# Key-value sums with the features stationary in four column groups, and small matmuls in groups of 32 tokens

## The chip, the core and the metric

The kernel runs on one core of one Trainium2 chip. The metric is the device time of one execution in microseconds; the figure for the kernel before is the median of three runs. A core has TensorE (PE, with its weight loads shown apart as PEld), VectorE (DVE), ScalarE (ACT), GpSimd (POOL) and SyncE (SP, which issues the transfers here). They run at the same time and wait for one another by semaphores.

## The reference

Two stages. The first is a linear attention over 4 batches, 4 heads, 1088 tokens and 32 dimensions. Each key and query is projected twice to 8 numbers, and the outer product of the two gives 64 features per head. The second is a gated feed-forward layer over all 4352 tokens, 128 wide, 2048 hidden.

```
phi(x)[i*8+j] = (S1 x)[i] * (S2 x)[j]          # 64 features per head
kv  = sum over tokens of phi(k) v^T            # 64 x 32 per batch and head
z   = sum over tokens of phi(k)                # 64 per batch and head
x   = (phi(q) kv) / (phi(q) z + 1e-6)
h   = x @ w_in ;  g = h * clip(h + 3, 0, 6) / 6 ;  out = g @ w_out
```

## The kernel before

**The feed-forward layer** takes most of the time. Tokens come in chunks of 512 (`CHUNKS`, eight of them and a last of 256), hidden features in pairs of 128-wide tiles. A step (`step`) multiplies a chunk by one pair of tiles of `w_in`. Both operands are split into a high and a low part, and three products are added: `L810` high by high, `L811` and `L816` the two cross terms. ACT adds 3 and clips below (`L823`), DVE clips above and multiplies (`L826`), ACT rounds to the high part (`L830`), and POOL or DVE subtracts to get the low part (`L834`). Three more products (`L855`, `L856`, `L858`) add the step to the output chunk. These six matmuls, 128 by 128 by 512, are called main matmuls below.

**The attention** feeds it. Per batch, the keys come in two groups of four and five tiles of 128 tokens (`KGROUPS`). `features` projects them: `L462` takes 64 tokens at a time as the stationary operand, two column groups of TensorE's array per tile, with the 64 projection columns moving. ACT copies the result (`L471`), DVE or POOL forms the outer products (`L490`).

Then the sums over the tokens (`keys`). Batch 0 (`b < DIRECT`) uses `kv_direct`, `L546`: a head's 64 features are stationary, in two column groups of 64, and 33 columns of v move, 32 of them the values and the last a column of ones, so that the 33rd result is z. Batches 1 to 3 use `kv`, `L561`: 32 columns of v are stationary, one column group of 32 per head, and the head's 64 features move, which gives kv turned on its side. For these batches z comes another way. `zz` (`L575`) sums the outer product of the two projections over all pairs of heads, `twice` copies kv and this product to SBUF on ACT (`L579`, `L581`), `turn` transposes kv (`L585`) and spreads the product to 128 partitions (`L588`, two matmuls with `spread` stationary), and `z` on DVE multiplies by a 0/1 matrix `pickT` and adds along the row (`L593`, `L596`). `spread` and `pickT` are made once near the start by `picks`, `turn_picks` and `copy_picks` (`L514`, `L516`, `L521`, `L524`). `halves` copies the result into `kvb[b]` on ACT (`L620`).

**The queries.** The first two chunks (`c < NEAR`) are transposed on TensorE (`L716`, copied at `L722`), the later ones (`far_queries`) by DVE and two transfers through DRAM; their projection is `L467`. The quotient is `nd` in `divided` (`L644`): 64 tokens at a time stationary, in two column groups, against `kvb`; DVE divides (`L651`, `L653`, `L655`). Then x is turned (`L672` or `L776`), and split (`L685`, `L689`).

**The order.** All of this is laid down as operations with an estimated cost per engine, a due time and the buffers they hold. `Plan.order` walks through modelled time and puts on each engine, whenever it is free, the ready operation with the earliest due time; the order that comes out is emitted as each engine's fixed queue. The due times are `when` and `xneed` minus the numbers in `LEADS`, `DUES`, `LOAD_DUE` and so on. Until `FILL_UNTIL` the plan puts filler matmuls (`L337`) where TensorE would be idle. An operation that may run on POOL or DVE is placed by `choose`, with `HOLD`, `SOON` and `PATIENCE`.

An fp32 matmul shows in the trace as two weight loads and two matmuls, so 144 rows of `L462` keys are 72 calls.

Of the kernel before, what the change touches and what calls it, by code (L numbers as in the profile page):

```python
# [15 lines left out]
F32 = mybir.dt.float32  # L16
# [3 lines left out]
ALU = mybir.AluOpType  # L20
# [56 lines left out]
BUFS = dict(h=2, o=2, a=2, raw=4, kT=3, v=3, qT=3, ab=3, kph=2, qph=2, phT=2, x=2, xh=5, g=5, gh=4, gl=4, os=2, part=4, cv=2, den=2, rden=2, xturn=1, xT=2, own=1, z=1, kvT=1)  # L77
ANY = ("a", "h", "o")

DIRECT = 1  # L80
# [7 lines left out]
DUES = (103.17, -33.21, 264.39, 135.8)  # L90
LAG = 103.99
W_DUE = (-192.19, 97.55, -48.18, 47.22, 162.42, -80.89, -2.9, 95.45)
CONV_LEAD = (-95.46, -154.15, 221.22, 172.43, 163.86, -1.9, 118.07, 58.88, -1.91)
LOAD_DUE = {'kT_0': -98.0, 'wiraw0': -99.0, 'kT_1': -96.0, 'kT_3': -92.0, 'qT_1': -95.0, 'v_3': -89.0, 'v_0': -93.0, 'qT_0': -97.0, 'v_1': -94.0, 'woraw0': -91.0, 'v_2': -88.0, 'kT_2': -87.0, 'wiraw1': -90.0}
LEADS = ({'ab': 12.96, 'cp': -82.47, 'ph': 183.6, 'kv': 105.14, 'kvb': 263.66, 'tr': 8.1, 'trcp': -338.67, 'nd': -150.04, 'norm': -67.61, 'xt': 144.32, 'xh': -299.21, 'xl': 20.48, 'k0': -50.53, 'kld': 93.74, 'vld': -73.42, 'qld': -227.7, 'rd': 94.61, 'xw': 73.75, 'xr': 86.41, 'sum': 208.48}, {'ab': 78.08, 'cp': 355.85, 'ph': -42.74, 'kv': 21.15, 'kvb': -73.24, 'tr': -268.31, 'trcp': -123.46, 'nd': -4.6, 'norm': 104.98, 'xt': 7.02, 'xh': -59.73, 'xl': 215.84, 'k0': 17.93, 'kld': -11.45, 'vld': 94.8, 'qld': 37.13, 'rd': 150.19, 'xw': 265.05, 'xr': -157.89, 'sum': -169.58}, {'ab': -313.33, 'cp': -208.9, 'ph': 497.08, 'kv': -430.54, 'kvb': 92.37, 'tr': 61.5, 'trcp': 1.64, 'nd': 28.0, 'norm': 109.69, 'xt': 35.9, 'xh': -102.84, 'xl': -39.8, 'k0': 445.75, 'kld': 300.46, 'vld': -93.89, 'qld': -26.76, 'rd': 164.41, 'xw': -289.67, 'xr': -28.97, 'sum': 42.05})


PICKS = 12.0


HOLD = 2.46
HOLD_DUE = -94.44
# [203 lines left out]
def fused_kernel(ctx: ExitStack, tc: tile.TileContext, qT, kT, v1, sb, w_in, w_out, outT):  # L306
# [18 lines left out]

    spread = const.tile([P, H, R, R], F32, name="spread")
    pickT = const.tile([P, 2, Q], F32, name="pickT")
# [122 lines left out]
    def features(src, n, name, tag, due, ld, srcb, psb, eng_cost, LEAD, far=False):  # L450


        T = {}
        pb, abb, phb = Buf(psb), Buf(("ab",)), Buf((tag,))
        T["abb"], T["n"] = abb, n

        def mm(_):
            T["ps"] = bank(pb.tag, f"abps_{name}")
            for t in range(n):
                out = T["ps"][:, : n * AB].rearrange("p (s x) -> p s x", s=2)[:, :, t * Q : (t + 1) * Q]  # L460
                for e in (0, HP):
                    nc.tensor.matmul(out[e : e + HP], src[0][:, t * P + e : t * P + e + HP], s_ab.rearrange("p s h r -> p s (h r)"), start=True, stop=True)  # L462
# [29 lines left out]
        if far:  # L492
            o1 = plan.add({PE: 0.1 + 0.121 * n}, due - LEAD["ab"], [ld], mm_far, [srcb, pb, abb], 256 * n, S_READY)
            o2 = plan.add({DVE: 0.12 + 0.067 * n}, due - LEAD["cp"], [o1], cp_far, [pb, abb])
        else:
            o1 = plan.add({PE: 0.11 + 0.115 * n}, due - LEAD["ab"], [ld], mm, [srcb, pb, abb], 256 * n, S_READY)
            o2 = plan.add({ACT: 0.06 + 0.0535 * n}, due - LEAD["cp"], [o1], cp, [pb, abb])
# [11 lines left out]
    turned = {}  # L509

    def picks(_):
        eye = ident[:Q, :Q].rearrange("k (h r) -> k h r", r=R)
        for e in range(0, P, Q):
            nc.scalar.copy(spread[e : e + Q], ident[e : e + Q, e : e + Q].rearrange("k (h r) -> k h r", r=R).unsqueeze(3).broadcast_to([Q, H, R, R]))  # L514
        turned["pick"] = buf("x", [P, 4, DM], "pick")[:Q, :2, :].rearrange("k t (h r s) -> k (t h) r s", r=R, s=R)
        nc.scalar.copy(turned["pick"], eye.unsqueeze(2).broadcast_to([Q, H, R, R]))  # L516

    def turn_picks(_):
        turned["ps"] = bank(pickb.tag, "pick_ps")
        for p in range(2):  # L520
            nc.tensor.transpose(turned["ps"][:, p * Q : (p + 1) * Q], turned["pick"][:, 2 * p : 2 * p + 2].rearrange("k h i j -> k (h i j)"), ident[:Q, :Q])  # L521

    def copy_picks(_):
        nc.scalar.copy(pickT, turned["ps"][:, : 2 * Q].rearrange("p (a x) -> p a x", a=2))  # L524

    pickb, turnedb = Buf(ANY), Buf(("x",))
    a = plan.add({ACT: 0.66}, PICKS, [], picks, [turnedb])
    a = plan.add({PE: 0.2}, PICKS, [a], turn_picks, [pickb, turnedb], 64)
    pick_op = plan.add({ACT: 0.16}, PICKS, [a], copy_picks, [pickb])

    def keys(b, due, psbs, ph_eng):
# [6 lines left out]
        def kv_direct(_, t, i, T, vbox):  # L538
# [4 lines left out]
            for h in range(H):  # L543
                w = slice(h * DV, (h + 1) * DV)
                e = F * (h % 2)
                nc.tensor.matmul(  # L546
                    K["ps"][e : e + F, w],
                    T["ph"][:rows, t, h * F : (h + 1) * F],
# [7 lines left out]
        def kv(_, t, i, T, vbox):  # L556

            if i == 0:
                K["ps"] = bank(kvbuf.tag, f"kvps_{b}")
            for h in range(H):  # L560
                nc.tensor.matmul(  # L561
                    K["ps"][h * D : (h + 1) * D, :F],
                    vbox[0][:, t, h * DV : h * DV + D],
                    T["ph"][:, t, h * F : (h + 1) * F],
                    start=i == 0,
                    stop=i == KT - 1,
                    tile_position=(0, h * D),
                )

        def zz(_, n, i0, T):  # L570

            for t in range(n):
                a, b_ = (T["ab"][:, x + t * Q : x + (t + 1) * Q] for x in (0, n * Q))
                e, i = t % 4 * Q, i0 + t
                nc.tensor.matmul(K["ps"][e : e + Q, Z0 : Z0 + Q], a, b_, start=False, stop=i >= KT - 4, skip_group_check=True, tile_position=(0, e))  # L575

        def twice(_):
            K["kvT"] = buf("kvT", [P, 2, F], f"kvT_{b}")
            nc.scalar.copy(K["kvT"], K["ps"][:, :F].unsqueeze(1).broadcast_to([P, 2, F]))  # L579
            K["z"] = buf("z", [P, Q], f"z_{b}")  # L580
            nc.scalar.copy(K["z"], K["ps"][:, Z0 : Z0 + Q])  # L581

        def turn(_):

            nc.tensor.transpose(K["ps"][:, P : 2 * P], K["kvT"].rearrange("p a f -> p (a f)"), ident)  # L585
            for p in range(2):
                at = Z0 + Q + p * Q
                nc.tensor.matmul(K["ps"][:, at : at + Q], spread[:, 2 * p : 2 * p + 2].rearrange("k h i j -> k (h i j)"), K["z"], start=True, stop=True)  # L588

        def z(_):  # L590

            own = buf("own", [P, 2, Q], f"own_{b}")
            nc.vector.tensor_tensor(own, K["ps"][:, Z0 + Q : Z0 + 3 * Q].rearrange("p (a x) -> p a x", a=2), pickT, op=ALU.mult)  # L593
            for u in range(2):
                at = u * DV + D
                nc.vector.tensor_reduce(kvb[b][u * F : (u + 1) * F, :, at : at + 1], own[u * F : (u + 1) * F], axis=mybir.AxisListType.X, op=ALU.add)  # L596

        for half in range(2):
# [5 lines left out]
            T, o3, phb = features(kbox, n, f"k{g}", "kph", d, lk, kb, psbs[half], ph_eng[half], LEAD)  # L604
            for t in range(n):
                i = t0 + t - b * KT
                mm = kv_direct if b < DIRECT else kv
                prev = plan.add({PE: 0.25 if b < DIRECT else 0.135}, d - LEAD["kv"] + 0.3 * t, [o3[t], lv, prev], partial(mm, t=t, i=i, T=T, vbox=vbox), [phb, vb, kvbuf], 528)
            if b >= DIRECT:
                prev = plan.add({PE: 0.1 + 0.04 * n}, d - LEAD["kv"] + 0.3 * n, [prev], partial(zz, n=n, i0=t0 - b * KT, T=T), [T["abb"], kvbuf], 32 * n)  # L610

        def halves(_):
            for e in (0, F):
                if b >= DIRECT:
                    at = P + e // F * D
# [328 lines left out]
```

## Time and profile before

| | us |
|---|---|
| median of three runs | 243.69 (243.48 to 243.83) |
| profiled execution | 244.41 |
| its span on the core | 242.3 |
| PE busy | 235.5 |
| DVE busy | 189.2 |
| ACT busy | 166.1 |
| POOL busy | 138.1 |

The span is the time from the first to the last instruction that the profiler saw; the profiled execution's own time holds 2.1 us more around it. Busy time is the time in which at least one instruction of the engine was running. A matmul's end is modelled, so the distance between the starts of two matmuls says more than their durations. The chain of waits follows the work that ended last back from the end: to what released an instruction, or to the instruction before it on its engine.

### The profile page before, as it was taken

What the parts mean: (1) busy time and instruction counts of PE and PEld (TensorE: products, weight loads), DVE (VectorE), ACT (ScalarE), POOL (GpSimd) and SP (SyncE); (2) the same over time, 40 slices, a digit from 0 to 9 for tenths busy, and PEclk for the clock granted to TensorE, in tenths of its full rate; (3) what the DMA queues carried; (4) which work ended last, traced back from release to release, by engine and by line L of the source; (5) the groups of instructions that cost most, each with busy time, mean ns of one, the idle gap of its engine ahead of it and who ended that gap; (6) DMA issues with size and microseconds to landing.
All of it is one profiled execution on the core that took longest, in us unless ns stands there. A gap on an engine that the chain in (4) does not pass through costs nothing.

```text
span 242.3 us, 4487 instructions
## 1 busy us (share of the span) xinstructions
PE 235.5 (97%) x1742; PEld 182.7 (75%) x1744; DVE 189.2 (78%) x261; ACT 166.1 (69%) x216; POOL 138.1 (57%) x86
## 2 busy tenths in 40 slices
PE   8998999999999989999999999999999999999994
PEld 3786767867767767787777777888788878888894
DVE  3899999999999999885664968766846495768771
ACT  6664798748756265689875865685678577768671
POOL 2734999966999936029976431254359704425400
PEclk9999999999999999999999999999999999999999
DMA  6998922014249965640000111410130010001010
GB/s 200 387 391 287 351 92 91 0 16 157 80 121 261 282 167 175 161 144 0 3 0 0 43 43 47 91 39 3 43 87 0 3 43 0 0 3 43 0 43 23
DMA packets 18004, 23.75 MB, mean 98 GB/s; under 512 B 1728, under 2 KB 11072, under 8 KB 17984
## 3 DMA queue, kind: packets, MB, share of 16 engines
q1 hardware_dynamic: 17984, 23.48, 30.7%
q8 instruction: 13, 0.21, 0.3%
q14 instruction: 7, 0.06, 0.1%
HBM read 16.26 MB, written 7.21 MB: 97 GB/s over the span
## 4 chain that ended last, share of the span: by engine, by line
PE 89%; DVE 8%; ACT 1%; issue 1%; DVEq 0%
PE o L855 13%; PE h L810 13%; PE o L856 13%; PE o L858 12%; PE h L816 12%; PE h L811 12%; PE nd L644 3%; PE warm L337 3%; DVE g L826 2%; PE abps_k L462 2%; PE kvps L561 2%; DVE gl L834 1%; PE abps_q L467 1%; PE kvps L546 1%; PE phps L716 1%
## 5 line engine op out<-in xcount | busy, mean ns | idle before, releaser
L834 POOL TENSOR_TENSOR gl<-g,gh 128x1024 fp32r<-128x1024 f32 (+1 forms) x42 | 100.2, 2399 | 73.4 <-ACT gh L830 28.5
L826 DVE SCALAR_TENSOR_TENSOR g<-g,h 128x1024 f32<-128x1024 f32 (+1 forms) x72 | 82.4, 1155 | 33.0 <-ACT g L823 31.7
L823 ACT ACTIVATE g<-h 128x1024 f32<-128x1024 f32 (+1 forms) x72 | 70.0, 978 | 32.2 <-PE h L816 21.2
L830 ACT CAST gh<-g 128x1024 fp32r<-128x1024 f32 (+1 forms) x72 | 72.0, 1001 | 24.6 <-PE o L856 18.3
L810 PE MATMUL h<-xh,wi_hi 128*128 128x512 f32 (+1 forms) x144 | 56.5, 393 | 1.9 <-DVE g L826 1.6
L855 PE MATMUL o<-gh,wo_hi 128*128 128x512 f32 (+1 forms) x144 | 55.6, 388 | 0.0
L811 PE MATMUL h<-xh,wi_lo 128*128 128x512 f32 (+1 forms) x144 | 55.0, 382 | 0.0
L816 PE MATMUL h<-xl,wi_hi 128*128 128x512 f32 (+1 forms) x144 | 55.0, 384 | 0.0
L856 PE MATMUL o<-gh,wo_lo 128*128 128x512 f32 (+1 forms) x144 | 54.6, 382 | 0.0
L858 PE MATMUL o<-gl,wo_hi 128*128 128x512 f32 (+1 forms) x144 | 43.7, 385 | 0.0
L834 DVE TENSOR_TENSOR gl<-g,gh 128x1024 fp32r<-128x1024 f32 (+1 forms) x30 | 36.2, 1214 | 5.6 <-ACT gh L830 5.3
L810 PEld LDWEIGHTS h<-xh,wi_hi 128*128 128x128 f32 x144 | 27.0, 187 | 10.0 <-DVE g L826 2.0
L855 PEld LDWEIGHTS o<-gh,wo_hi 128*128 128x128 f32 x144 | 27.0, 188 | 6.6 <-ACT gh L830 0.5
L816 PEld LDWEIGHTS h<-xl,wi_hi 128*128 128x128 f32 x144 | 27.0, 188 | 5.8
L856 PEld LDWEIGHTS o<-gh,wo_lo 128*128 128x128 f32 x144 | 27.0, 188 | 5.3
L811 PEld LDWEIGHTS h<-xh,wi_lo 128*128 128x128 f32 x144 | 27.0, 188 | 5.0
L858 PEld LDWEIGHTS o<-gl,wo_hi 128*128 128x128 f32 x144 | 26.0, 188 | 5.6
L490 POOL TENSOR_TENSOR ph_k<-ab_k 128x512 f32<-128x512 f32 (+1 forms) x15 | 14.6, 988 | 11.0 <-ACT ab_k L471 11.0
L490 POOL TENSOR_TENSOR ph_q<-ab_q 128x512 f32<-128x512 f32 x14 | 16.8, 1218 | 4.1 <-DVE ab_q L475 2.0
L644 PEld LDWEIGHTS nd<-kvb,phT 128*64 128x64 f32 x272 | 9.2, 137 | 4.0 <-issue 2.7
L644 PE MATMUL nd<-kvb,phT 128*64 128x66 f32 x272 | 11.0, 226 | 0.0
L748 DVE STREAM_TRANSPOSE pht<-ph_q 128x1024 f32<-128x1024 f32 (+1 forms) x7 | 8.1, 1158 | 0.1
(87 smaller groups left out, 171.5 us busy)
## 6 DMA issues: line engine op xcount, KB each, us to landing
phd<-pht SPq DMA_DIRECT2D x24, 128.0 KB, 3.5
phT<-phd SPq DMA_DIRECT2D x6, 512.0 KB, 4.4
wiraw<-w_in_dram SPq DMA_DIRECT2D x4, 512.0 KB, 6.9
qT<-qT_dram SPq DMA_DIRECT2D x8, 256.0 KB, 5.8
woraw<-w_out_dram SPq DMA_DIRECT2D x4, 512.0 KB, 5.4
outT_dram<-os SPq DMA_DIRECT2D x8, 256.0 KB, 2.0
xd<-xt SPq DMA_DIRECT2D x24, 64.0 KB, 1.9
xT<-xd SPq DMA_DIRECT2D x6, 256.0 KB, 2.8
```

What stands on the lines that cost most here:

```text
L490: engines[e].tensor_tensor(out, a_, b_, op=ALU.mult)
L644: nc.tensor.matmul(W["nd"][e : e + HP, o : o + 2 * DV], T["phT"][:, p, i : i + HP], kvb[batch_of(c0 + i)][:, p, :], start=True, stop=True)
L810: nc.tensor.matmul(T["h"][:, u, :n], wi_hi[:, f], x, start=True, stop=False)
L811: nc.tensor.matmul(T["h"][:, u, :n], wi_lo[:, f], x, start=False, stop=False)
L816: nc.tensor.matmul(T["h"][:, u, :n], wi_hi[:, f], x, start=False, stop=True)
L823: nc.scalar.activation(T["g"][:, :, :n], T["h"][:, :, :n], AF.Relu, bias=3.0, scale=1.0)
L826: nc.vector.scalar_tensor_tensor(T["g"][:, :, :n], T["g"][:, :, :n], 6.0, T["h"][:, :, :n], op0=ALU.min, op1=ALU.mult)
L830: nc.scalar.copy(T["gh"][:, :, :n], T["g"][:, :, :n])
L834: engines[e].tensor_tensor(T["gl"][:, :, :n], T["g"][:, :, :n], T["gh"][:, :, :n].bitcast(F32), op=ALU.subtract)
L855: nc.tensor.matmul(o, wo_hi[:, f], T["gh"][:, u, :n], start=first and u == 0, stop=False)
L856: nc.tensor.matmul(o, wo_lo[:, f], T["gh"][:, u, :n], start=False, stop=False)
L858: nc.tensor.matmul(o, wo_hi[:, f], T["gl"][:, u, :n], start=False, stop=last and u == 1)
```

## The change

All batches now use one form of the sums over the tokens. A head's 64 features are stationary in two halves of 32, so that four column groups of 32 are used, and the 33 columns of v with the ones move. One token tile takes eight calls in place of four. `DIRECT`, `kv_direct`, `zz`, `twice`, `turn`, `z`, the pick matrices and their buffers (`own`, `z`, `kvT`) are gone, and `halves` is the same for all batches.

The keys of batches 1 to 3 and the quotients of chunks 2 to 8 take 32 tokens at a time in four column groups, where they took 64 in two; batch 0's keys, all of `L462`'s queries and the first two chunks' quotients stay as they are. The planner's costs of these operations are changed, and all of its due times, leads and holds; among the loads, qT_0 goes from third to tenth place and woraw0 from ninth to last of the thirteen named ones. The copies of the projections and the outer products of the features are not changed.

```diff
-STEP = 6.61
-DUES = (103.17, -33.21, 264.39, 135.8)
-LAG = 103.99
+STEP = 4.6
+DUES = (154.74, -15.16, 342.66, 122.47)
+LAG = 20.51
...
-LOAD_DUE = {'kT_0': -98.0, 'wiraw0': -99.0, 'kT_1': -96.0, 'kT_3': -92.0, 'qT_1': -95.0, 'v_3': -89.0, 'v_0': -93.0, 'qT_0': -97.0, 'v_1': -94.0, 'woraw0': -91.0, 'v_2': -88.0, 'kT_2': -87.0, 'wiraw1': -90.0}
+LOAD_DUE = {'kT_0': -98.0, 'wiraw0': -99.0, 'kT_1': -97.0, 'kT_3': -89.0, 'qT_1': -96.0, 'v_3': -95.0, 'v_0': -94.0, 'qT_0': -90.0, 'v_1': -93.0, 'woraw0': -87.0, 'v_2': -88.0, 'kT_2': -92.0, 'wiraw1': -91.0}
...
-HOLD = 2.46
+HOLD = 21.82
...
-    def features(src, n, name, tag, due, ld, srcb, psb, eng_cost, LEAD, far=False):
+    def features(src, n, name, tag, due, ld, srcb, psb, eng_cost, LEAD, far=False, w=HP):
...
-                for e in (0, HP):
-                    nc.tensor.matmul(out[e : e + HP], src[0][:, t * P + e : t * P + e + HP], s_ab.rearrange("p s h r -> p s (h r)"), start=True, stop=True)
+                for e in range(0, P, w):
+                    nc.tensor.matmul(out[e : e + w], src[0][:, t * P + e : t * P + e + w], s_ab.rearrange("p s h r -> p s (h r)"), start=True, stop=True)
...
-        def kv_direct(_, t, i, T, vbox):
+        def kv(_, t, i, T, vbox):
...
-            for h in range(H):
+            for h, f in product(range(H), range(0, F, Q)):
                 w = slice(h * DV, (h + 1) * DV)
-                e = F * (h % 2)
+                e = F * (h % 2) + f
                 nc.tensor.matmul(
-                    K["ps"][e : e + F, w],
-                    T["ph"][:rows, t, h * F : (h + 1) * F],
+                    K["ps"][e : e + Q, w],
+                    T["ph"][:rows, t, h * F + f : h * F + f + Q],
                     vbox[0][:rows, t, w],
...
-            T, o3, phb = features(kbox, n, f"k{g}", "kph", d, lk, kb, psbs[half], ph_eng[half], LEAD)
+            T, o3, phb = features(kbox, n, f"k{g}", "kph", d, lk, kb, psbs[half], ph_eng[half], LEAD, w=Q if b else HP)
...
-                prev = plan.add({PE: 0.25 if b < DIRECT else 0.135}, d - LEAD["kv"] + 0.3 * t, [o3[t], lv, prev], partial(mm, t=t, i=i, T=T, vbox=vbox), [phb, vb, kvbuf], 528)
-            if b >= DIRECT:
-                prev = plan.add({PE: 0.1 + 0.04 * n}, d - LEAD["kv"] + 0.3 * n, [prev], partial(zz, n=n, i0=t0 - b * KT, T=T), [T["abb"], kvbuf], 32 * n)
+                prev = plan.add({PE: 0.14}, d - LEAD["kv"] + 0.3 * t, [o3[t], lv, prev], partial(kv, t=t, i=i, T=T, vbox=vbox), [phb, vb, kvbuf], 528)
...
+            w = HP if c < NEAR else Q
+            for u, p, e in product(range(m), range(2), range(0, P, w)):
                 o = (2 * u + p) * 2 * DV
                 i = (t + u) * P + e
-                nc.tensor.matmul(W["nd"][e : e + HP, o : o + 2 * DV], T["phT"][:, p, i : i + HP], kvb[batch_of(c0 + i)][:, p, :], start=True, stop=True)
+                nc.tensor.matmul(W["nd"][e : e + w, o : o + 2 * DV], T["phT"][:, p, i : i + w], kvb[batch_of(c0 + i)][:, p, :], start=True, stop=True)
```

More of the change, by code (lines that the diff above doesn't have):

```diff
@@ L74 @@
 FILL_UNTIL = 17.0
-BUFS = dict(h=2, o=2, a=2, raw=4, kT=3, v=3, qT=3, ab=3, kph=2, qph=2, phT=2, x=2, xh=5, g=5, gh=4, gl=4, os=2, part=4, cv=2, den=2, rden=2, xturn=1, xT=2, own=1, z=1, kvT=1)
+BUFS = dict(h=2, o=2, a=2, raw=4, kT=3, v=3, qT=3, ab=3, kph=2, qph=2, phT=2, x=2, xh=5, g=5, gh=4, gl=4, os=2, part=4, cv=2, den=2, rden=2, xturn=1, xT=2)
 ANY = ("a", "h", "o")
-DIRECT = 1
 CONV_BANK = ("a", "h", "o")
@@ L108 @@
+HOLD = 21.82
+HOLD_DUE = -27.43
+SOON = 22.85
+SOON_DUE = 316.94
+PATIENCE = 0.75
 @dataclass(eq=False)
@@ L324, in fused_kernel @@
     make_identity(nc, ident)
-    spread = const.tile([P, H, R, R], F32, name="spread")
-    pickT = const.tile([P, 2, Q], F32, name="pickT")
     kvb = []
@@ L495, in features @@
         else:
-            o1 = plan.add({PE: 0.11 + 0.115 * n}, due - LEAD["ab"], [ld], mm, [srcb, pb, abb], 256 * n, S_READY)
+            o1 = plan.add({PE: 0.11 + 0.115 * n if w == HP else 0.13 + 0.1 * n}, due - LEAD["ab"], [ld], mm, [srcb, pb, abb], 256 * n, S_READY)
             o2 = plan.add({ACT: 0.06 + 0.0535 * n}, due - LEAD["cp"], [o1], cp, [pb, abb])
@@ L507, in fused_kernel @@
     kv_done = {}
[L509 to L529, printed above, removed]
     def keys(b, due, psbs, ph_eng):
@@ L554, in kv_direct @@
                 )
[L556 to L596, printed above, removed]
         for half in range(2):
@@ L622, in keys @@
-        if b >= DIRECT:
-            kvTb, zb = Buf(("kvT",)), Buf(("z",))
-            a = plan.add({ACT: 0.37}, due - LEAD["kvb"] - 1.0, [prev], twice, [kvbuf, kvTb, zb])
-            prev = plan.add({PE: 0.8}, due - LEAD["kvb"] - 0.5, [a, pick_op], turn, [kvbuf, kvTb, zb], 400)
-            rest = [plan.add({DVE: 0.45}, due - LEAD["kvb"], [prev, pick_op], z, [kvbuf, Buf(("own",))])]
-        else:
-            rest = []
-        kv_done[b] = [plan.add({ACT: 0.43}, due - LEAD["kvb"], [prev], halves, [kvbuf]), *rest]
+                src = K["ps"][e : e + F, : 4 * DV].rearrange("p (a x) -> p a x", a=2)[:, :, e // F * DV : (e // F + 1) * DV]
@@ L631, in fused_kernel @@
+                at = e // F * DV
+                nc.scalar.copy(kvb[b][e : e + F, :, at : at + DV], src)
+        kv_done[b] = [plan.add({ACT: 0.43}, due - LEAD["kvb"], [prev], halves, [kvbuf])]
     x_t, x_ops, x_buf = {}, {}, {}
@@ L640, in nd @@
             W["nd"] = bank(nb.tag, f"nd_{c}_{t}")
-            for u, p, e in product(range(m), range(2), (0, HP)):
+            w = HP if c < NEAR else Q
+            for u, p, e in product(range(m), range(2), range(0, P, w)):
                 o = (2 * u + p) * 2 * DV
                 i = (t + u) * P + e
-                nc.tensor.matmul(W["nd"][e : e + HP, o : o + 2 * DV], T["phT"][:, p, i : i + HP], kvb[batch_of(c0 + i)][:, p, :], start=True, stop=True)
+                nc.tensor.matmul(W["nd"][e : e + w, o : o + 2 * DV], T["phT"][:, p, i : i + w], kvb[batch_of(c0 + i)][:, p, :], start=True, stop=True)
         def norm(_):
@@ L657, in divided @@
         batches = range(batch_of(c0), batch_of(c0 + n - 1) + 1)
-        a = plan.add({PE: 0.05 + 0.27 * m}, due - LEAD["nd"] - lag, [ready, *(o for b in batches for o in kv_done[b])], nd, [phTb, nb, xb], 528 * m)
+        a = plan.add({PE: 0.08 + 0.27 * m if c < NEAR else 0.08 + 0.23 * m}, due - LEAD["nd"] - lag, [ready, *(o for b in batches for o in kv_done[b])], nd, [phTb, nb, xb], 528 * m)
         return plan.add({DVE: 0.56 + 0.1 * m}, due - LEAD["norm"] - lag, [a], norm, [nb, xb])
```

19 lines of the change are left out of this document (3 added, 16 removed).

## The prediction

> **What bounds the kernel now.** I read the page's head first: busy shares, slices, and the chain that ended last.
>
> ```profile
> span 242.3 us, 4487 instructions
> ...
> PE 235.5 (97%) x1742; PEld 182.7 (75%) x1744; DVE 189.2 (78%) x261; ACT 166.1 (69%) x216; POOL 138.1 (57%) x86
> ...
> PE   8998999999999989999999999999999999999994
> ...
> DVE  3899999999999999885664968766846495768771
> ...
> PEclk9999999999999999999999999999999999999999
> ...
> GB/s 200 387 391 287 351 92 91 0 16 157 80 121 261 282 167 175 161 144 0 3 0 0 43 43 47 91 39 3 43 87 0 3 43 0 0 3 43 0 43 23
> ...
> PE 89%; DVE 8%; ACT 1%; issue 1%; DVEq 0%
> ```
>
> TensorE is busy throughout at full clock, and 89% of the chain is its own queue. But DVE is also at nine tenths or more in slices 3 to 16, to about 97 us (a slice is 242.3 / 40 = 6.06 us). Whether TensorE time saved early is worth anything depends on that, so I split the span into stretches.
>
> ```profile
> 30.00:50.00 20.00, 19.95 (x102) 15.07 (x102) 19.94 (x32) 16.17 (x23) 20.00 (x11) 1.00 0.17 57
> 50.00:75.00 25.00, 25.00 (x235) 18.02 (x235) 24.40 (x39) 16.44 (x23) 20.64 (x14) 1.00 0.39 100
> ```
>
> (Columns: stretch, length, busy PE, PEld, DVE, ACT, POOL, clock, DMA share, GB/s.) From 30 to 50 us PE, DVE and POOL are all full; from 50 us POOL has 4.4 us free in 25; after 109 us the slices show PE alone full.
>
> Next, what a visit to the attention work costs TensorE, from the chain in order of time (start, length, what):
>
> ```profile
> 100.30 0.47 PE o L858 x2
> 100.77 0.58 PE kvps L561 x32
> 101.35 0.43 PE h L810
> ```
>
> A main matmul takes 0.23 us on the chain (two in 0.47), the first one after a visit 0.43: going out and back costs about 0.20 beside the small matmuls. So a visit that vanishes returns its own time and 0.20; work that vanishes inside a visit returns its own time alone.
>
> **The pace of the small matmuls.** An fp32 matmul shows as two weight loads and two matmuls; I call each load with its matmul a pair. Timeline (start, length of the merged stretch) and groups by shape:
>
> ```profile
> 52.03 0.54 PE L561 MATMUL kvps<-ph_k,v 128*32 128x64 f32 x24
> 52.39 0.24 PE L575 MATMUL kvps<-ab_k 128*32 128x32 f32 x8
> ```
>
> ```profile
> L561 PE MATMUL kvps<-ph_k,v 128*32 128x64 f32 x216 | 5.1, 223 | 0.4 <-issue 0.4
> L546 PE MATMUL kvps<-v,ph_k 128*64 128x33 f32 x64 | 2.1, 224 | 0.2 <-ACT phT L722 0.2
> L575 PE MATMUL kvps<-ab_k 128*32 128x32 f32 x54 | 1.6, 196 | 0.0
> ```
>
> A stretch less one duration, over the steps in it, is the pace. Four groups of 32, 64 moving columns (L561): (0.54 - 0.22) / 23 = 14 ns per pair. Four groups of 32, 32 moving columns (L575): (0.24 - 0.196) / 7 = 6.3 ns; between 6 and 8, as the rows are rounded to 10 ns.
>
> **The change, part by part.** Ramp and visit rows from the same chain:
>
> ```profile
> 6.52 0.24 PE pick_ps L521 x2
> ...
> 7.37 0.47 PE abps_q L462 x16
> ...
> 11.31 2.41 PE kvps L546 x72
> 13.72 1.02 PE phps L716 x8
> ...
> 22.98 0.06 PE kvps L575 x8
> ```
>
> *(a) Batch 0's kv.* Now 72 pairs, two groups of 64, take 2.41 us, 0.268 per token tile. New: per tile 4 heads x 2 halves x 2 passes = 16 pairs of 32 stationary and 33 moving columns, 144 in all. This shape is not in the trace. Bounds: 7 ns per pair (L575, same stationary, 32 columns) gives 1.0 us, and 14 ns (L561, 64 columns) 2.0. The shape is nearest to L575, so 7.3 ns, a little more for the 33rd column and the roundings: 1.05 us, gain **1.36** (0.4 to 1.4). It stands on the chain (next comes L716).
>
> *(b) Later kv.* 27 tiles: 8 pairs at 14 ns (0.112 us) become 16 pairs at 7.3 ns (0.117): **+0.1** (up to 16 x 14 = 0.224 per tile, +3.0).
>
> *(c) Outer products for the sums (L575).* Five of six hang on a kv visit, 0.06 each as at 22.98. One stands alone:
>
> ```profile
> 120.02 0.24 PE kvps L575 x10
> 120.27 0.43 PE o L855
> ```
>
> It costs 0.24 + 0.20 = 0.44. Gain 5 x 0.06 + 0.44 = **0.74** (0.3 if the lone visit's place is taken by other work).
>
> *(d) The turns (L585, L588).* One of three lies wholly on TensorE:
>
> ```profile
> 60.94 0.61 PE abps_k L462 x16
> 61.56 0.26 PE kvps L585
> 61.82 0.37 PE kvps L588 x4
> 62.18 0.31 PE h L810
> ```
>
> 0.26 + 0.37 + 0.31 - 0.43 (the way back that abps_k would pay anyway) = **0.51**. The other two fill time in which TensorE then waits for DVE (the first turn lies between the first two of these rows, the second begins the third):
>
> ```profile
> 28.01 0.69 PE L462 MATMUL abps_k<-s_ab,kT 128*64 128x64 f32 x16
> ...
> 29.76 0.50 PE L810 MATMUL h<-xh,wi_hi 128*128 128x512 f32 x1 [0.44 <-DVE g L826]
> ...
> 144.66 0.27 PE L585 MATMUL kvps<-ident,kvT 128*128 128x128 f32 x1
> ...
> 145.66 0.48 PE L810 MATMUL h<-xh,wi_hi 128*128 128x512 f32 x1 [0.36 <-DVE g L826]
> ```
>
> They go for 0: the main matmul behind them waits longer for the same gate. If the wait goes too, each is worth what lies from 144.66 to 145.66, about 1.0.
>
> *(e) Later keys and quotients in groups of 32.* A key group of four tiles, now 16 pairs, becomes 32 pairs of exactly L561's shape: 0.58 (100.77) in place of 0.61 (60.94), so 0.03 to 0.04. Six groups of batches 1 to 3 give 0.2. A quotient operation of two tiles, likewise 16 pairs with 66 moving columns, becomes 32; its row:
>
> ```profile
> 64.59 0.62 PE nd L644 x16
> ```
>
> 0.62 against 0.59 (0.58 scaled by 66 / 64 on the matmul part), 0.03 for each of the 13 operations of chunks 2 to 8: 0.35. Together **0.55** (0 to 0.7).
>
> *(f) Off TensorE.* Gone are five copies on ACT for the pick matrices and pickT, six copies for kvT and z, and on DVE a product and two reductions per batch:
>
> ```profile
> L593 DVE TENSOR_TENSOR own<-kvps,pickT 128x64 f32<-128x64 f32 x3 | 0.7, 217 | 0.0
> ...
> L596 DVE TENSOR_REDUCE kvb<-own 64x2 f32<-64x64 f32 x6 | 1.3, 217 | 0.1
> ...
> 7.42 0.37 ACT L471 COPY ab_k<-abps_k 128x256 f32<-128x256 f32 x1 [0.41 <-PE abps_k L462]
> ```
>
> DVE loses 0.7 + 1.3 = 2.0 us. I take 0 for both engines: ACT waits 0.41 us for TensorE after the picks, and DVE's gain counts only if DVE is the bound (a rival). pick_ps on TensorE (0.24) goes for 0 too: behind it abps_k waits for its keys to land, so that load is late next. Bound 0.24.
>
> *(g) The order.* Every due time, lead and hold of the planner changes, and the loads: qT_0 moves from third to tenth, behind 2.27 MB more by the tiles' shapes. At the 387 GB/s of a full slice that is 5.9 us; its product, now at 7.37, would come at about 13.3. With its copy and outer product
>
> ```profile
> L490 DVE TENSOR_TENSOR ph_q<-abps_q,ab_q 128x512 f32<-128x512 f32 x2 | 1.4, 676 | 0.0
> ```
>
> its transposes would come at 13.3 + 0.47 + 0.37 + 0.68 = 14.8; today the later of the first two chunks has them at 13.72. qT_1 is now ahead of it, so chunk 1 can go first. I take 0, with 1.1 as the loss if chunk 0 gates. woraw0 becomes the last of the named thirteen loads; late next would be the first output matmul, which waits for its conversion. One visit more or fewer shifts the time by 0.20 or a little more; I take their number as unchanged.
>
> **Sum** against the profiled execution, 244.41 us (span 242.3 and 2.1 around it): 1.36 - 0.1 + 0.74 + 0.51 + 0.55 = 3.1, so 241.3. That execution is 0.7 above the median of the runs, 243.69, from which it is **240.6**.
>
> **Rivals.**
>
> *DVE takes the saving before 97 us.* For it: DVE is full there, and the chain runs over it for most of 25 to 31 us, ending so:
>
> ```profile
> 30.31 1.13 DVE g L826
> ...
> 31.48 0.50 PE h L810
> ```
>
> Against: DVE takes correction products (L834) that POOL could do, and POOL is 17% free from 50 us. What is left: the lone sum visit 0.44, seven quotient operations after 90 us (at 90.7, 92.5 and 196 us, and two each at 150 and 172) 0.2, and DVE's two early turns, 2 x 0.65 = 1.3. Sum 1.9: **241.8**.
>
> *A pair's pace doesn't follow its moving columns.* Place: every kv tile. For it: two groups of 64 run no faster with 33 columns than with 64: (2.41 - 0.22) / 71 = 31 ns for L546, (0.69 - 0.22) / 15 = 31 ns for L462 at 28.01. And L575 shows its 6 ns over eight to ten pairs, not over 80. Against: L575 itself, and that two groups of 64 load the same 128 columns whatever moves, which alone would make them equal. At 14 ns the sum is 0.4 - 3.0 + 0.74 + 0.51 + 0.55 = -0.8: **244.5**, slower. It decides from 3.1 us / 576 pairs = 5.4 ns over 7.3, that is 12.7 ns per pair. The Trainium skill speaks for this rival: TensorEngine Tiling, section Instruction Overhead, says that each matmul has some 60 cycles of overhead, that a free dimension of 1 takes as long as one of 60, and that no tiling should be taken from a dimension that is already small. By it 33 columns would cost like L561's 64 and the kernel would end at 244.5; the row of L575, 32 columns at half the pace of 64, disagrees.
>
> *Instruction supply.* The kernel gets some 530 pairs more. In the densest stretch TensorE stops in the middle of a kv tile, with no releaser:
>
> ```profile
> 23.63 0.31 PE L561 MATMUL kvps<-ph_k,v 128*32 128x64 f32 x6 [0.39 <-issue]
> ```
>
> 0.39 us idle, and some 0.1 to refill the array: four more of them: 240.6 + 4 x 0.5 = **242.6**. Against: the 32 pairs quoted at 52 us run through without one.
>
> *The waits go too.* The two turns' 1.0 each are won as well, in a new order without these gates: 240.6 - 2.0 = **238.6**.
>
> *The new order is worse*: chunk 0 gates the ramp (1.1) and eight visits more, kv tiles one by one, each 0.20 or more (1.8): 240.6 + 2.9 = **243.5**. For it: each tile is an operation of its own, free to be placed apart; against: the chain shows them at 100.77 and elsewhere in one piece of four.
>
> **Chances.** Forecast 0.42 (239.6 to 241.5), DVE 0.21, pace 0.07, supply 0.11, waits gone 0.12, worse order 0.07. Range 238.3 to 243.3: it leaves out the pace rival, most of the worse order and little at the low end. About 0.2% (0.5 us) is what a measurement of this kernel can tell from none. Faster: 0.42 + 0.21 + 0.10 + 0.12 = 0.85; same 0.05, of the worse order and of supply; slower 0.10, pace and the rest.
>
> **What would show it.** kvps by form: 128x33 pairs at 7 ns, batch 0's stretch near 1.05 us (right for a, b); at 14 ns the pace rival. No L575, L585, L588 rows. abps_k x32 in 0.58, nd x32 in 0.59 on the chain. First h before 19 us if the ramp gain is real; if it stays at 19.7 and h waits for DVE more than now, the DVE rival. "issue" stops inside tiles: supply. The prediction is wrong if the pairs keep 12.7 ns, or if the chain shows more DVE than 8% and the end is above 242.

## The result: 0.6% slower, and the profile after

The changed kernel takes 245.3 us (median of 7 runs, 244.57 to 246.56) beside 243.83 us (7 runs, 243.48 to 244.62) for the kernel before: a ratio of 1.0059, with a 95% interval of 1.0033 to 1.0086. The prediction, 240.6 with a range to 243.3, was wrong in sign. The profiled execution took 245.6 us with a span of 243.4. Of e9 and e13 below, the profile is of a slower execution that the comparisons leave out, so these two are used for their first 26 us and for the places of stops alone; e13 has one comparable time, 244.18 us, beside 248.28, 248.75 and 249.77.

The head of the page after:

```profile
span 243.4 us, 5531 instructions
...
PE 234.9 (97%) x2281; PEld 182.4 (75%) x2281; DVE 183.0 (75%) x251; ACT 163.3 (67%) x204; POOL 141.7 (58%) x87
...
PEclk9967999999999999999999999999999999999999
...
PE 91%; issue 2%; DMA 2%; ACT 2%; DVE 1%; SPq 0%
```

TensorE has 539 more matmul rows and yet is busy 0.6 us less. DVE fell from 8% of the chain to 1%. New are 2% of "issue" and the third and fourth digit of the clock: between 12 and 24 us TensorE did not run at full speed. The chain in order of time shows why (start, length, what):

```profile
9.45 0.70 PE kvps L514 x59
10.14 0.59 PE phps L629 x4
10.73 0.95 PE kvps L514 x75
11.68 0.48 PE phps L629 x3
12.16 3.41 issue
15.57 0.47 PE phps L629
16.05 1.01 PE abps_k L452 x32
17.06 1.96 PE nd L557 x32
...
24.33 0.23 PE h L723
```

TensorE stops for 3.41 us between the third and the fourth of four transposes that wait for nothing; then everything goes at half speed. The stretches give the clock and the DMA share (columns as in the prediction), after and then before:

```profile
10.00:15.00 5.00, 2.16 (x103) 1.63 (x89) 2.58 (x5) 1.00 (x3) 0.28 (x1) 0.92 1.04 383
15.00:20.00 5.00, 4.42 (x82) 3.92 (x83) 2.28 (x7) 1.49 (x4) 2.09 (x2) 0.50 1.06 409
20.00:25.00 5.00, 5.00 (x64) 3.29 (x64) 4.31 (x8) 3.68 (x7) 1.82 (x2) 0.89 0.55 167
```

```profile
10.00:15.00 5.00, 4.76 (x100) 4.27 (x100) 4.97 (x9) 3.21 (x8) 2.61 (x3) 1.00 1.05 386
15.00:20.00 5.00, 4.60 (x103) 3.85 (x100) 4.69 (x14) 3.25 (x7) 2.69 (x3) 1.00 1.05 407
```

The first main matmul starts at 24.09 us after and at 19.72 before, from the two timelines:

```profile
24.09 0.48 PE L723 MATMUL h<-xh,wi_hi 128*128 128x512 f32 x1
```

```profile
19.72 0.47 PE L810 MATMUL h<-xh,wi_hi 128*128 128x512 f32 x1 [0.24 <-DVE x L655]
```

So the start-up lost 4.4 us. The rest won 3.3: I added up, from the starts of consecutive main matmuls, all distance beyond 0.234 us (0.116 in the last chunk), and got 28.4 us before and 25.1 after. 4.4 - 3.3 = 1.1 is the difference of the spans, 243.4 - 242.3.

**What the stop is.** The queue that the page calls "instruction" carries packets of 16,384 bytes, 13 before and 18 after:

```profile
q8 instruction: 18, 0.29, 0.5%
```

I numbered every record of TensorE and its queue from the start, semaphore records too. In every kernel below, the stops inside a group fall at number 449 + 256 k (in profiles that lack a record or two: at 448, or 703): the program comes in blocks of 256, and 16,384 / 256 is 64 bytes each. The packets of the later part of a run start near record 200 + 256 k (after 60 us nearly all within 64 records of it), so I take that as the time when a block is asked for; it is an estimate. Worked out from the trace's records for the first such block:

```
kernel   record 200 at  packet from  to      449 goes on at
before       11.37        13.93     14.81    no stop
after         9.60        13.21     14.15    15.57
```

After, TensorE asks 1.8 us earlier, because batch 0's kv begins at 9.38 us there and at 11.31 before. The packet starts 3.6 us later, while the DMA engines are full with loads (share 1.04), and TensorE goes on 1.4 us after the packet's end. But with twice the instructions in batch 0's kv, TensorE went from record 200 to the last one ahead of 449 in 2.3 us, by 11.9, and then stood. Before, the block is late too, 2.6 us, but TensorE needs 4.7 us, until 16.1, to get to record 449. That is the theory to be tested; it is the third rival of the prediction, instruction supply, with another price.

### The profile page after: what moved, and what is told of

Read it like the earlier page. It is cut to its first block, busy times and chain, and to the rows that moved or that the text cites. A ratio compares the mean times of both kernels' runs of the same rounds, so it can differ in the third digit from the quotient of the medians.

```text
span 243.4 us, 5531 instructions
## 1 busy us (share of the span) xinstructions
PE 234.9 (97%) x2281; PEld 182.4 (75%) x2281; DVE 183.0 (75%) x251; ACT 163.3 (67%) x204; POOL 141.7 (58%) x87
## 4 chain that ended last, share of the span: by engine, by line
PE 91%; issue 2%; DMA 2%; ACT 2%; DVE 1%; SPq 0%
PE h L723 14%; PE h L729 13%; PE o L771 13%; PE o L768 13%; PE h L724 13%; PE o L769 13%; PE nd L557 4%; PE kvps L514 3%; DMA kT<-kT_dram 2%; PE abps_k L452 2%; PE abps_q L457 2%; PE phps L629 1%; PE warm L326 1%; ACT g L736 1%; PE abps_q L452 1%
## 5 line engine op out<-in xcount | busy, mean ns | idle before, releaser
L747 POOL TENSOR_TENSOR gl<-g,gh 128x1024 fp32r<-128x1024 f32 (+1 forms) x45 | 106.4, 2373 | 65.1 <-ACT gh L743 60.4
L768 PE MATMUL o<-gh,wo_hi 128*128 128x512 f32 (+1 forms) x144 | 55.0, 384 | 0.0
L747 DVE TENSOR_TENSOR gl<-g,gh 128x1024 fp32r<-128x1024 f32 (+1 forms) x27 | 31.5, 1171 | 1.7 <-ACT gh L743 1.5
L480 POOL TENSOR_TENSOR ph_q<-ab_q 128x512 f32<-128x512 f32 x13 | 13.7, 1069 | 3.5 <-DVE ab_q L465 3.5
L557 PEld LDWEIGHTS nd<-kvb,phT 128*32 128x32 f32 (+1 forms) x480 | 9.3, 119 | 3.6 <-issue 3.1
L602 POOL TENSOR_TENSOR xl<-xT,xh 128x512 fp32r<-128x512 f32 x4 | 6.2, 1550 | 9.0 <-ACT xh L598 9.0
L557 PE MATMUL nd<-kvb,phT 128*32 128x66 f32 (+1 forms) x480 | 11.2, 229 | 0.0
```

Source lines behind the costliest of these rows:

```text
L480: engines[e].tensor_tensor(out, a_, b_, op=ALU.mult)
L557: nc.tensor.matmul(W["nd"][e : e + w, o : o + 2 * DV], T["phT"][:, p, i : i + w], kvb[batch_of(c0 + i)][:, p, :], start=True, stop=True)
L747: engines[e].tensor_tensor(T["gl"][:, :, :n], T["g"][:, :, :n], T["gh"][:, :, :n].bitcast(F32), op=ALU.subtract)
L768: nc.tensor.matmul(o, wo_hi[:, f], T["gh"][:, u, :n], start=first and u == 0, stop=False)
```

## Experiments

The theory: what decides is when TensorE reaches the end of a block in the first 30 us, while that block's transfer waits behind the loads. Its rivals: the new order, the data being late, and the narrow kv itself.

**e1: batch 0's kv in two groups of 64 again.** The changed kernel with one edit:

```diff
-            for h, f in product(range(H), range(0, F, Q)):
+            G = Q if b else F
+            for h, f in product(range(H), range(0, F, G)):
...
-                    K["ps"][e : e + Q, w],
+                    K["ps"][e : e + G, w],
```

> The changed kernel, with batch 0's kv alone back in two groups of 64 features (72 pairs for 144); the planned order is the same. Theory (instruction supply): TensorE's instructions come in blocks of 256 (16 KB), and a block that is asked for while the loads fill the DMA queues comes some 6 us later; the changed kernel used up its blocks at 11.9 us and stood for 3.4 us, and the clock then fell to half for 6.8 us. With 144 instructions fewer the end of the second block is reached only after 15 us, when the next one is there: no stop above 0.6 us, clock 1.00 in every stretch from 15 to 25 us, first h at 18.5 to 20.5 us in place of 24.1, ratio to the kernel before 0.984 to 0.992. Rival (the new order of the loads and of the ramp is what is slow): first h stays at 23 to 24 us, ratio 1.000 to 1.006.

Measured: 247.18 us, ratio 1.0152 (1.0130 to 1.0174), slower still. The first main matmul comes at 19.82, as the theory had it, with a stop of 0.50 us left at record 449, but the total missed, because the long stops moved to the next two blocks, into batch 1's kv. Timeline, and the stretch with its clock:

```profile
23.79 0.35 PE L515 MATMUL kvps<-v,ph_k 128*32 128x33 f32 x18 [1.44 <-issue]
...
27.89 0.32 PE L515 MATMUL kvps<-v,ph_k 64*32 64x33 f32 x3 [1.94 <-issue]
```

```profile
25.00:30.00 5.00, 3.06 (x111) 2.81 (x99) 1.82 (x4) 2.37 (x5) 2.13 (x3) 0.77 0.71 199
```

These are records 705 and 961. Batch 0 alone is not the cause; the narrow work that comes next meets a full queue too (DMA share 1.01 from 20 to 25 us).

**e2: only batch 0's kv narrow, in the kernel before.**

```diff
-            for h in range(H):
+            for h, f in product(range(H), range(0, F, Q)):
...
-                e = F * (h % 2)
+                e = F * (h % 2) + f
```

> The kernel before, with batch 0's kv alone in four groups of 32 features (144 pairs for 72); order, loads and all other work as before. Theory (instruction supply): a stop of 2 to 4 us in or right behind batch 0's kv, half clock after it, first h at 21.5 to 24.5 us in place of 19.7, ratio 1.006 to 1.020. Rival (the shape itself is as good as forecast and the loss lies in the order): kv takes 1.3 us in place of 2.4, first h at 18.5 to 19.5, ratio 0.994 to 0.998.

Measured: 248.24 us, ratio 1.0170 (1.0143 to 1.0196). The chain:

```profile
11.12 1.35 PE kvps L546 x114
12.47 3.14 issue
15.61 0.51 PE kvps L546 x18
```

With the old order and the old loads, 72 pairs more make the same stop, at record 449, here in the middle of a token tile; the first main matmul comes at 23.09. So neither the new order nor the other parts of the change are needed for it. The kv itself is faster than in two groups (1.35 + 0.51 us on the chain for 2.41), and the kernel 4.5 us slower.

**e3: e1, and keys and quotients back to 64 tokens.**

```diff
-            T, o3, phb = features(kbox, n, f"k{g}", "kph", d, lk, kb, psbs[half], ph_eng[half], LEAD, w=Q if b else HP)
+            T, o3, phb = features(kbox, n, f"k{g}", "kph", d, lk, kb, psbs[half], ph_eng[half], LEAD, w=HP)
...
-            w = HP if c < NEAR else Q
+            w = HP
```

> As the kernel with batch 0's kv in groups of 64, and besides all keys and quotients in groups of 64 tokens; only the later kv stays in groups of 32. Prices the groups of 32 tokens: by the rows of the changed kernel a quotient of two tiles takes 0.453 + 0.15 us in place of 0.470 + 0.15, a key group 0.435 in place of 0.463, and the way in is 0.02 shorter each time, so this kernel is slower than the one with batch 0 alone undone by 0.3 to 0.7 us (ratio higher by 0.001 to 0.003). Rival: 320 pairs fewer relieve the instruction supply, and it is the same or faster by up to 0.6 us.

Measured: 247.38 us, ratio 1.0151 (1.0135 to 1.0167), as e1, where 0.3 to 0.7 us more were expected. Two effects stand against each other: with fewer instructions the stops in the first 30 us are down to 0.43 and 0.33 us and the clock is full, but TensorE now waits for other engines in an order that was laid out for other costs:

```profile
32.26 0.47 PE L724 MATMUL h<-xh,wi_hi 128*128 128x512 f32 x1 [1.50 <-DVE g L740]
```

So e3 says nothing on the price of the 32-token groups.

**e4, e5, e6: lighter loads.** Five early loads bring a sixteenth of their columns, and POOL fills the rest with ones, in the changed kernel (e4, and again with more runs in e5) and in the kernel before (e6).

```diff
+LIGHT = ("wiraw1", "woraw0", "woraw1", "kT_2", "kT_3")
...
+            if name in LIGHT:
+                nc.gpsimd.memset(t.bitcast(F32), 1.0)
+                d, k = (view(t) if view else t), slice(0, src.shape[-1] // 16)
+                nc.sync.dma_start(d[..., k], src[..., k])
+                return
```

> The changed kernel with five early loads (the second block of w_in, the first two of w_out, the keys of groups 2 and 3) cut to a sixteenth of their columns; the rest of those tiles is set to 1.0 by POOL, so these weights and keys are left out of the computation. TensorE's work and order are the same. Theory (the instruction block waits behind the loads): the instruction fetch starts within 1 us of the 200th TensorE instruction (in the changed kernel 3.6 us after it), the stop at 11.9 us is under 1 us, the clock stays at 1.00, first h before 21 us. Rival (the fetch takes its 5 to 6 us whatever the loads do): the stop stays at 3 us or more.

> The changed kernel with five early loads cut to a sixteenth (second block of w_in, first two of w_out, keys of groups 2 and 3; the rest of those tiles is 1.0, so these weights and keys are left out), timed. One look gave a span of 240.3 us with three stops of 0.9 to 1.0 us left, where the blocks end. Theory (instruction supply): repeated, 242.0 to 243.0 us, 2.5 to 3.5 below the changed kernel with all its loads.

> The kernel before with the same five loads cut to a sixteenth: the control for the changed kernel with light loads. Theory (the change saves TensorE work, and the loads' hold on the instruction blocks turns it into a loss): the kernel before has one stop of 0.6 us at its third block, which goes, and otherwise gains little: 242.6 to 243.6 us, so that with light loads the changed kernel is the faster one by 0.5 to 2 us. Rival (light loads help both alike, the change is a loss in itself): the kernel before falls to 241 us or below and stays ahead of the changed one.

Measured: e4 242.42 us in a single run; e5 242.45, ratio 0.9948 (0.9920 to 0.9976), where the full loads had 1.0059; e6 245.93, ratio 1.0081 (1.0046 to 1.0116), where 242.6 to 243.6 us were expected. The same stop, in e4 and in e5:

```profile
13.03 0.33 PE L635 MATMUL phps<-ident,ph_q 128*128 128x128 f32 x1 [0.71 <-issue]
```

```profile
13.80 0.33 PE L635 MATMUL phps<-ident,ph_q 128*128 128x128 f32 x1 [1.54 <-issue]
```

With not one instruction of TensorE changed, 3.41 us became 0.71 and 1.54, and 2.9 us came off. In e5 the stop of 1.54 us was still followed by half clock, for 3.4 us (14.64 to 18.05). e6 was to show what the lighter loads give by themselves. It is no clean control: POOL's fills stand ahead of its own early work there, and the first main matmul came 0.8 us later than before (20.53). So how much of the 2.9 us is the stop, and how much is data that landed earlier, these three leave open.

**e10 to e13: the same loads, later.** A copy of one element on ACT into a load's buffer makes that load, and all behind it on SP's queue, wait. The gate stands ahead of the second block of w_in (e10, e12) or of the load after it (e11, e13), and opens with batch 0's second copy of projections (e10, e11) or with its last outer product (e12, e13). No work is left out, and no queue's order changes.

```diff
+            if name == GATED:
+                nc.scalar.copy(t.bitcast(F32)[:1, :1], gate["ab"][:1, :1])
             nc.sync.dma_start(view(t) if view else t, src)
...
-    for op in plan.order():
+    ops = plan.order()
+    i, j = ops.index(gate["load"]), ops.index(gate["copy"])
+    late = [op for op in ops[i:j] if op.engine == SP]
+    rest = [op for op in ops[i : j + 1] if op.engine != SP]
+    for op in ops[:i] + rest + late + ops[j + 1 :]:
```

> The changed kernel with all of its work and every engine's order kept; the loads from the second block of w_in on are issued only after batch 0's second copy of key projections (about 8.0 us; they were issued from 5.2 us on), by a copy of one element into that block's buffer on ACT. Instruction supply: by the tiles' shapes, the loads ahead of the gate hold 2.65 MB, and the changed kernel's trace had moved 2.64 MB by 9.6 us, where the block for instruction 449 is asked for. So its transfer starts by about 10.5 us in place of 13.2, TensorE stops at index 449 for 0.7 us or less in place of 3.7, the clock isn't halved, and the first main matmul comes at about 20.3 in place of 24.1; 241.6 us (240.8 to 242.8), with one further stop of up to 1 us at index 705. Rival, that the loads and not the instructions set the start: they land some 3 us later than before the gate, TensorE waits for them, first main matmul at 24 or later, 245 or more.

> As e10_gate_w_in, but the second block of w_in (512 KB) is still issued at 5.2 us; the gate stands ahead of the next load. Instruction supply: 3.17 MB ahead of the gate have moved by about 11.0 us at the rate of the trace (0.39 MB per us), so the block's transfer starts at about 11 to 11.5, TensorE resumes at about 13.5 and the stop at index 449 is 1.2 to 1.8 us; first main matmul about 21.5; 242.8 us (242 to 244), between e10_gate_w_in and the changed kernel. Rival, loads set the start: no earlier than the changed kernel, 245.

Measured: e10 246.09 us, ratio 1.0085 (1.0061 to 1.0110); e11 245.1, ratio 1.0056 (1.0031 to 1.0080). Both missed; their times are those of the rival, but TensorE stood at record 449 again, not at a wait for a load. The stop in e10's chain:

```profile
13.08 3.37 issue
```

In e10 SP issued the first load behind the gate at 9.17 us and three more by 10.5, just ahead of the time at which the block was asked for (10.52). That left two readings: the block waits behind these, or for something that has nothing to do with loads.

> As e10_gate_w_in, but the gate opens only when batch 0's last outer product of the keys is done (10.6 us in the changed kernel), behind the time at which the block for instruction 449 is asked for (9.6 us). In e10_gate_w_in the gate opened at 9.2, and the block, asked for at about 10.5, still began at 14.2. If the block waits behind the loads: it now finds its queue empty and begins at about 10 to 10.8, TensorE stops at index 449 for under 0.5 us, with no half clock, and the first main matmul comes before 21; the loads themselves are 4 to 5 us late, so the time is 241.5 to 244.5. If it waits for something else than the loads, it begins at 13 to 14 again, and TensorE stops for 3 us or more.

> As e12_gate_w_in_later, but the second block of w_in is still issued at 5.2 us, so 3.17 MB stand ahead of the gate, moved by about 11. If the block waits behind the loads, it begins at about 10.5 to 11.3, TensorE stops for 0.7 to 1.5 us at index 449, and the first main matmul comes at about 21; 241.5 to 244. If it waits for something else, it begins at 13 to 14, with a stop of 3 us, as in e11_gate_qT.

Measured: e12 246.33 us, ratio 1.0093 (1.0056 to 1.0129); e13 244.18. Both times missed, but the block's start went as the first reading had it. The stop in e12 and in e13:

```profile
14.61 0.33 PE L639 MATMUL phps<-ident,ph_q 128*128 128x128 f32 x1 [1.14 <-issue]
```

```profile
13.34 0.33 PE L639 MATMUL phps<-ident,ph_q 128*128 128x128 f32 x1 [0.69 <-issue]
...
20.03 0.48 PE L733 MATMUL h<-xh,wi_hi 128*128 128x512 f32 x1
```

All six in one table, from the records (the stop is the row's idle time):

```
                 record 200 at   packet from   wait   stop
after                 9.60          13.21      3.6    3.41
e10 gate, early      10.52          14.19      3.7    3.37
e11 gate, early       9.88          13.13      3.3    3.05
e12 gate, late       10.91          11.93      1.0    1.14
e13 gate, late       10.09          11.17      1.1    0.69
e5  light loads       9.70          11.38      1.7    1.54
```

With the loads held back past record 200, the block starts 1.0 to 1.1 us after it is asked for in place of 3.6 (in e12 the DMA share is 0.08 or less from 10.5 to 11.5 us), the clock stays at 1.00 from 10 to 20 us, and e13 has its first main matmul at 20.03 in place of 24.09. So the block does wait behind loads already queued. The price is that these are late in their turn. In e12 TensorE waits 1.93 us for ACT, which stands at the conversion of the first block of w_out (`mag_wo`), whose transfer ends on the chain after 20 us. The clock is halved from 23.08 to 26.49, here behind a wait for ACT and not for instructions, and the first main matmul comes at 24.26:

```profile
13.71 6.97 DMA woraw<-w_out_dram
...
20.77 0.67 ACT mag_wo L344
...
21.46 0.65 PE abps_q L465 x4
```

In e13's profile the loads that were held back fill the queues when the third block is due (DMA share 1.03 from 20 to 25 us): asked for at 19.3, its packet starts at 25.6, and TensorE stops at record 961. There, moving the loads moved the stop. No profile here has the changed kernel's full work without a long stop or a long wait in its place.

**e7: of the whole change only the quotients of chunks 2 to 8 at 32 tokens,** in the kernel before, which puts no instruction more into the first 60 us.

```diff
-            for u, p, e in product(range(m), range(2), (0, HP)):
+            w = HP if c < NEAR else Q
+            for u, p, e in product(range(m), range(2), range(0, P, w)):
```

> The kernel before with one part of the change alone: the quotients of chunks 2 to 8 in groups of 32 tokens (208 pairs more, all after 60 us, where the loads leave the instruction blocks free). Theory: 13 operations gain 0.017 each in the run of pairs and 0.02 on the way in, 0.3 to 0.6 us in all, ratio 0.997 to 0.999, and no stop at a block's end. Rival (more instructions cost time everywhere): 1.000 to 1.004.

Measured: 242.88 us (10 runs, 242.16 to 243.19), ratio 0.9948 (0.9931 to 0.9964). It beats both kernels, by more than expected, and gives more than its rows: a quotient operation costs up to 0.02 us less, all 13 about 0.2. The rest of the 1.2 us between the two profiled spans is, by the distances between main matmuls, a wait of 0.8 us at 87 us that is gone, less 0.3 for one that is longer at 102, and the stop of 0.3 at 23 us that is absent, which instructions after 60 us can't have caused. Timelines, before and e7:

```profile
86.58 0.32 PE L561 MATMUL kvps<-ph_k,v 128*32 128x64 f32 x8
87.68 0.50 PE L810 MATMUL h<-xh,wi_hi 128*128 128x512 f32 x1 [0.78 <-DVE g L826]
```

```profile
86.12 0.32 PE L561 MATMUL kvps<-ph_k,v 128*32 128x64 f32 x8
86.37 0.50 PE L811 MATMUL h<-xh,wi_hi 128*128 128x512 f32 x1
```

Why that wait is gone was not tested.

**e8: e7, and batches 2 and 3 with narrow kv and keys,** their sums and turns dropped where they stood in the old order.

```diff
+NARROW = 2
...
-            rows = min(P, S - i * P)
+            rows = P if b >= NARROW else min(P, S - i * P)
+            G = Q if b >= NARROW else F
...
-                if b >= DIRECT:
+                if DIRECT <= b < NARROW:
```

> The kernel before, in its own order, with the change where the loads have ended: quotients of chunks 2 to 8 in groups of 32, and batches 2 and 3 with keys in groups of 32 and the features stationary in four groups (sums, copies and turns of these two batches dropped in place; the last tile with all 128 rows, zeros where there is no token). Batches 0 and 1 as before. Theory (the change is a gain wherever the instruction blocks arrive in time): against the kernel with the 32-token quotients alone another 0.3 to 1.0 us, ratio to the kernel before 0.990 to 0.994, no stop over 0.3 us at a block's end after 24 us. Rival (the kv pairs at 9 to 10 ns in place of 7 eat what the turns gave): 0.994 to 0.997.

Measured: 243.56 us, ratio 0.9982 (0.9968 to 0.9995): faster than before, but not than e7, so the expectation missed. It makes no stop after 24 us, where the DMA engines have room. The turn at 60.9 was worth 0.56 us, by the distance between the main matmuls around it. The turn at 144.66 was worth nothing; the main matmul behind it waits for the same gate as long as both took before:

```profile
143.12 0.63 PE L869 MATMUL o<-gl,wo_hi 128*128 128x512 f32 x2
144.59 0.47 PE L821 MATMUL h<-xh,wi_hi 128*128 128x512 f32 x1 [0.84 <-DVE g L837]
```

The wait at 86 that e7 was rid of is back (0.81 us), which takes what the turn gave.

**e9: e8 with batch 1 changed too** (`NARROW = 1`, the last tile of a batch at its 64 tokens).

> As the kernel with batches 2 and 3 changed in the order of the kernel before, but batch 1 changed too (its kv runs at 22 to 25 us, while the loads fill the DMA queues; 144 pairs for 72 and 18), and the last tile of each changed batch with its 64 rows. Batch 0 as before. Theory (instruction supply): the block that ends at 23 us in the kernel before ends earlier in it, a stop of 1 to 3 us at 21 to 25 us, ratio 0.998 to 1.010. Rival (only batch 0 is in the way): as fast as with batches 2 and 3 alone or faster, 0.988 to 0.994.

Measured: ratio 1.0112 (1.0062 to 1.0162) from three comparable times of 244.93 to 248.6 us, slower. Batch 1's kv lies at 22 to 30 us. Its stops are at records 705 and 961, as in e1. Between e8 and e9 the change turns from gain to loss, and what differs, besides the 64 rows of the last tiles, is narrow work while the loads are still coming.

## Why the prediction was wrong, point by point

**The step that failed is the price of instruction supply.** The prediction had the rival, "four more of them: 240.6 + 4 x 0.5", and gave it 0.11. The size came from the stop of 0.39 us at 23.63, a block that came just too late, with 0.1 for refilling the array that no row shows, and the argument against it from 32 pairs at 52 us, where the DMA share is 0.39 (its row of 50 to 75 us). Both rows are from places with a late block that TensorE barely overtook, or with free queues. The place that counted was 9 to 20 us: 144 pairs in 1.65 us where 72 had taken 2.41, with the DMA share at 1.04 to 1.06. One stop of 3.41 us and the half clock behind it came out there, not four of 0.5. The same three groups at half clock (timeline after) and at full clock (e12):

```profile
15.98 1.08 PE L452 MATMUL abps_k<-s_ab,kT 128*32 128x64 f32 x32
16.99 2.03 PE L557 MATMUL nd<-kvb,phT 128*64 128x66 f32 x32
18.81 1.07 PE L452 MATMUL abps_q<-s_ab,qT 128*64 128x64 f32 x16
```

```profile
14.87 0.65 PE L460 MATMUL abps_k<-s_ab,kT 128*32 128x64 f32 x32
15.46 1.16 PE L567 MATMUL nd<-kvb,phT 128*64 128x66 f32 x32
17.43 0.69 PE L460 MATMUL abps_q<-s_ab,qT 128*64 128x64 f32 x16 [0.82 <-DVE rden L576]
```

They differ by 0.43 + 0.87 + 0.38 = 1.7 us. 3.4 + 1.7 - 0.8, the true gain of (a), is 4.3, beside the 4.4 lost. The sum is rough, as the first keys came earlier too (see f); e13, with a stop of 0.69 us and full clock, shows the same size more directly: first main matmul 4.1 us earlier.

**(a), 1.36, was 0.8.** The pairs run at 9 ns, not 7.3. Timeline and groups after:

```profile
9.38 0.77 PE L514 MATMUL kvps<-v,ph_k 128*32 128x33 f32 x64
...
10.66 1.02 PE L514 MATMUL kvps<-v,ph_k 128*32 128x33 f32 x80
```

```profile
L514 PE MATMUL kvps<-v,ph_k 128*32 128x33 f32 x512 | 6.9, 198 | 0.4 <-issue 0.4
L514 PE MATMUL kvps<-v,ph_k 64*32 64x33 f32 x64 | 1.3, 197 | 0.0
```

(0.77 - 0.20) / 63 = 9.0 ns and (1.02 - 0.20) / 79 = 10.4 ns, together 1.40 us. The second stretch holds one step of 0.125 us, between the starts of two matmuls, where the last token tile with its 64 rows begins; without it the pace is 9.1 ns (before, that step is 0.153 in L546). The row of L575 gave the pace of ten pairs; it did not hold for 64. The prediction also set a product of pairs and pace against a stretch of the chain, which holds the way out as well. Like for like, the chain after has 0.70 + 0.95 = 1.65 us for what took 2.41: a gain of 0.8.

**(b), 0.1 loss, was 1.2.** The same 1.40 us stand against 9 tiles x 8 x 14 ns = 1.01 for a later batch, 0.4 for each of three. About 0.1 of each is the step at the 64-row tile: in the kernel before, all of L561's rows have 128.

**(c) and (d)** hold: the rows of L575, L585 and L588 are gone, the lone turn was worth 0.56 where 0.51 was predicted, and of the turns that fill a wait the one at 144.66 was worth 0 in the old order (e8); the one at 28 was not tried alone.

**(e)** gave 0.2 for the quotients (e7), where 0.35 was predicted. For the keys, groups of 32 and 40 pairs take 0.44 and 0.55 us, and 16 and 20 took 0.46 and 0.58 (worked out from starts): 0.03 each, as predicted.

**(f)** was too low in the ramp: it took 0 for the picks on TensorE because the first keys would still wait for their load, but these start at 5.98 after and at 6.68 before, and the second group, which does wait for its load, at 6.73 and 8.31. Batch 0's kv begins 1.9 us earlier, and the block's end comes earlier with it. **(g)** was priced at nothing. In the main stage the new order is better: (c), (d) and (e) less (b), 0.74 + 0.56 + 0.4 - 1.2, make 0.5 of the 3.3 us won there; the rest are waits. Before, those at 28, 31, 86, 102 and 144 us, with the turns that fill two of them, and the stop at 23 sum to about 3.7, by the distances between main matmuls; after, a wait at 41 and a stop at 32 leave 0.8. Which part of the new order took the waits away was not tested. So "the waits go too" came about as well, behind a start-up that ate it.

**The other rivals.** DVE takes the saving: no, DVE is 1% of the chain after. Pace that doesn't follow the moving columns: no, 9 ns with 33 columns beside 14 with 64. The Trainium skill's TensorEngine Tiling, section Instruction Overhead, would have them alike; the trace disagrees. Its advice not to take a tiling from a dimension that is already small points both ways here: the sums of batches 1 to 3 lost 1.2 us, and the quotients, also split from 64 to 32, gained 0.2 (e7).

## What to carry to other kernels

Count instructions, not only time: a tiling in narrower groups that saves time per tile can double the instructions per microsecond, and while loads fill the DMA queues the program itself arrives late. Price it in that stage, from the DMA share there, and count in the clock that falls after a long stop. Here narrow groups gained late in the kernel, where the queues are free (e7, about 0.2 us by its rows), and lost in the ramp (e2).

## What was not expected of the hardware

TensorE stopped between instructions that wait for nothing at records 449 + 256 k, for 0.3 to 3.4 us, in the first 33 us of these kernels. The packet of such a block took 0.9 to 1.4 us, and TensorE went on 1.2 to 1.6 us after its end. For the first block it started 1.0 to 1.1 us after record 200 with the loads held back (e12, e13) and 2.2 to 3.7 us after it with all loads in the queues. The Trainium skill, Runtime: NRT & Kernel Launch, section Instruction fetch mechanics, says that instructions come in blocks of 16 KiB, or 256, and that crossing a boundary is mostly hidden; the first agrees with the packets here, the second does not hold at the stops above, 3.41 us in the changed kernel.

After a stop of 3.41 us the granted clock was halved for 6.8 us (14.24 to 21.06 us in the clock's records), and stops of 1.44 and 1.94 us in e1 were followed by 0.77 in the stretch from 25 to 30 us. It was halved for 3.4 us behind stops of 3.37 (e10), 3.05 (e11) and 1.54 us (e5), and not behind the 1.14 us of e12.

Open is by what rule the DMA engines let the block in between the loads: in e10 and e11 a block still waited 3.7 and 3.3 us when the loads had been issued in the 1.2 to 1.4 us ahead of its time, and no run here measured how many of them go first.
